# New priority offsets for a planned attention and expert kernel, with the products of batch 2 moved to VectorE

## The chip, the cores and the metric

The kernel runs on one core of a Trainium2 chip. A time is the device time of one execution in microseconds (us). Before the change it is 289.33 us, the median of three runs (289.2, 289.33 and 290.66).

The core has five instruction streams that run side by side and each in their own order: TensorE (PE, with its weight loads shown as PEld), VectorE (DVE), ScalarE (ACT), GpSimd (POOL) and SyncE (SP). SP and POOL also issue transfers between memory and the core; the transfers themselves run on 16 DMA engines.

## What is computed

A gated linear attention feeds a small mixture of four experts. In the reference's words, cut:

```python
# attention: B, H, S, D = 4, 8, 768, 48
f = 1.0 / (1.0 + np.exp(-f_logit))
for t in range(S):
    state = f[:, :, t, :, None] * state + np.einsum('bhd,bhe->bhde', k[:, :, t], v[:, :, t])
    y[:, :, t] = np.einsum('bhd,bhde->bhe', q[:, :, t], state)
# experts: x is y as (B*S, H*D) = (3072, 384); w1 is (4, 384, 1024), w2 is (4, 1024, 384)
p = domain_probs / (domain_probs.sum(-1, keepdims=True) + 1e-09)
for e in range(E):
    h = np.maximum(x @ w1[e], 0.0)
    out += p[:, e:e + 1] * (h @ w2[e])
```

## The kernel before the change

The 768 time steps are cut into six chunks of 128. A chunk holds four batches, each a tile of 128 steps by 8 heads of 48. Inside a chunk the recurrence is written as products of matrices: the gates' logarithms are summed along time on PE, ACT takes exponentials of the sums, q and k are multiplied by these, transposed, and multiplied with each other; the state is carried from chunk to chunk. The result of a chunk (512 rows of x) goes through the four experts. From the second half of chunk 1 on, two experts are handled together in a form with seven products in place of eight. Matrix work is in bf16.

**The plan.** The kernel does not write its order by hand. It declares some 1,470 steps with a priority, a cost for each engine that may run it, its dependencies and the buffers that it takes and frees. `Plan.run` walks through time and gives each engine that is free the ready step of the lowest priority. The list it returns is emitted in that order, and this fixes two things: which engine runs a step that two could run, and the order of the steps on each engine. On the chip an engine executes its steps in that order and waits at the first one that is not ready. `MOVES` is a string of corrections: `q 0.2=3.2` adds 3.2 to the priority of the step named `q 0.2`, and `@DVE` behind a number also binds the step to that engine.

**Names of steps.** The first two numbers are chunk and batch.

- `ld f0.2`, `ld k0.2`, `ld q0.2`: loads of inputs, issued by SP (L282). The loads `v issue 0` to `v issue 3` of chunk 0 and the weight pieces `w issue 0` to `w issue 10` are issued by POOL (L278, L291) and convert to bf16 on the way. `w 0` is one half of expert 0's first matrix (384 KB as bf16), `w 1` the other half, `w 2` and `w 3` those of expert 1, `w 4` and `w 5` the halves of expert 0's second matrix; `w 6` to `w 10` are whole matrices of 768 KB.
- `gate1`, `gate2`, `cs`, `exps`: the gates on ACT, their running sums on PE (L319) and the exponentials `e` on ACT (L339).
- `q 0.2`, `k 0.2`: the products of q and k with the exponentials (L347), on DVE or POOL.
- `tpq`, `tpk`, `ev_tp`: transposes on PE (L356) and their copy out. From batch 2 of chunk 1 on, `tp` is a transposing transfer on SP's queue (L360).
- `at`, `ev_at0`, `ev_at1`, `y`: scores on PE (L383), masked on DVE (L387), and the chunk's result on PE (L394, L398).
- `ev_y`, `xt`, `ev_xt`: in chunk 0 and the first half of chunk 1, the copy of `y`, its transpose on PE and the copy out. Later `ev_ys` scales `y` by the experts' shares (L370 on ACT, L372 on DVE) and `xs` is a transposing transfer on SP's queue (L375).
- `kv`, `ev_kv`, `sf`: the update of the state (PE, DVE, POOL).
- `h 0.1.3.0`: chunk 0, expert 1, hidden block 3: x times w1 on PE (L432); `relu` its eviction (L441, L443). `o 0.1.2.0`: the result of expert 1 for batch 2 from the first half of the hidden blocks (`.1`: from the second half), L447; `ev_o` its eviction, and `store` the transfer to memory (L513).
- `hs`, `relu_s`, `s1` to `s4`, `p`, `ev_p`: the same for pairs of experts (L464, L472, L482, L501, L509 and L271).

**The beginning.** Until chunk 0's attention has made its first x, PE has little to do, and the kernel pads it with matrix products on a constant (L867). `first` is the first `h` step; the number of padding products ahead of each PE step is worked out from the plan's times:

```python
if o.engine == "PE" and o.start <= first:
    o.pad, t = int((o.start - t) / (0.42 if t < 7.0 else 0.25)), o.end
```

**POOL's order in the beginning** is `k 0.0`, `v issue 0`, `q 0.1`, `v issue 1`, `v issue 2`, `q 0.2`, `w issue 0`, `v issue 3`, `w issue 1` and so on to `w issue 9`. `v issue 0` waits for the landing of k of batch 1, `v issue 1` for that of batch 2 (`v_gate`). `w issue 10` waits for the landing of k of chunk 1.

Of the kernel before, what the change touches and what calls it, by code (L numbers as in the profile page):

```python
# [12 lines left out]


MOVES = (
    "q 0.2=3.2;k 0.3=-8.9;ev_y 0.3=-23.3@ACT;cs 1.0=0.8;k 1.0=-0.2;cs 1.1=-4.4;v 1.2=8@ACT;tp 1.2=-43.6;tp 1.3=-25;ev_xt 1.1=24.3;"
    "xs 1.3.1=7.9;ld v2.2=7.4;h 0.0.0.0=-7.3;relu 0.0.0.0=3.1@DVE;relu 0.0.2.0=10.6;relu 0.0.3.0=29@ACT;h 0.0.5.0=6.8;h 0.1.1.0=-16.7;"
    "h 0.1.2.0=-22.6;h 0.1.3.0=-119.1;o 0.1.1.1=4.2;o 0.1.3.0=11.3;h 0.3.2.0=-3.7;relu 0.3.3.0=-13.8@DVE;h 0.3.4.0=-12.9;o 0.2.2.0=28.6;"
    "o 0.2.3.0=-1.9;h 0.3.7.0=39.5;cs 2.1=31.3;tp 2.2=9.1;ev_at1 2.0=17;ev_ys 2.0.0.1=-0@ACT;ev_ys 2.1.1.0=-35.5@ACT;xs 2.1.1=12.6;"
    "ev_ys 2.2.0.1=-0.6@ACT;kv 2.2=48.1;ld k3.0=-2.9;o 0.3.2.1=2.1;store 0.3.0=22.7;h 1.0.0.0=-9.5;relu 1.0.4.0=-0.8@DVE;"  # L20
    "h 1.0.5.0=-42.9;h 1.1.0.0=-50.1;h 1.1.1.0=-41.2;h 1.1.2.0=-4;relu 1.1.2.0=-12.9@DVE;h 1.1.3.0=-41;h 1.1.4.0=-2.3;"
    "relu 1.1.6.0=-44.9@DVE;h 1.2.0.0=-1.9;h 1.2.1.0=-7.4;h 1.2.3.0=-7.1;relu 1.2.4.0=1.6@DVE;h 1.2.5.0=8.6;h 1.3.2.0=8;o 1.2.1.0=10.2;"
    "h 1.3.4.0=-11.3;h 1.3.5.0=-23.7;h 1.3.6.0=-11.9;hs 1.1.0.1.4=-1.2;relu_s 1.1.0.1.4=-9@ACT;hs 1.1.0.1.6=-6.4;hs 1.1.1.1.4=4.8;"
    "exps 3.0=7.9;k 3.1=-3.6;k 3.2=56.5;ev_ys 3.0.0.0=-1.5@DVE;ev_ys 3.0.0.1=0@ACT;ev_ys 3.0.1.0=44.9;ev_ys 3.1.0.0=50.8@DVE;"
    "ev_ys 3.1.0.1=0@ACT;ev_at1 3.2=7.6;ev_ys 3.3.1.0=0.1@DVE;ev_ys 3.3.1.1=6.1@DVE;ev_kv 3.0=23;kv 3.3=9.3;ev_kv 3.3=13.2;"
    "ld q4.0=-11.2;ld k4.2=26.7;ld q4.2=26.5;ev_p 1.1.1.1=6.4;hs 2.0.0.0.2=4.5;p 1.1.1.3=8.6;store 1.2.0=34.8;hs 2.0.0.0.6=-14.7;"
    "hs 2.0.0.1.6=2.4;s3 2.0.0=-32.1;hs 2.0.1.1.0=6.1;hs 2.0.1.0.4=-4.2;hs 2.0.1.1.4=2.8;relu_s 2.0.1.1.4=51.5;p 2.0.1.7=2.6;"
    "p 2.0.1.3=33.7;ev_p 2.0.1.4=-10.5;p 2.1.0.1=1.3;p 2.1.0.2=1.7;hs 2.1.1.0.2=-1.4;hs 2.1.1.1.2=-3.1;p 2.1.0.5=-17.1;"
    "hs 2.1.1.0.6=27.4;hs 2.1.1.1.6=-5.3;s2 2.1.1=-16.6;gate2 4.0=33.9;cs 4.0=-2.3;v 4.1=-8;ev_ys 4.0.0.0=5.6@DVE;ev_ys 4.0.0.1=44@DVE;"
    "xs 4.0.0=-37.1;ev_ys 4.0.1.0=-0@ACT;ev_at1 4.1=1.9;y 4.1=-4.7;ev_ys 4.1.0.1=3.8@DVE;ev_at0 4.3=-29.9;ev_ys 4.3.1.0=-16.5;"  # L30
    "ev_kv 4.1=-1.3;kv 4.2=15.9;ld q5.0=-19.7;ld v5.0=8.7;ld k5.2=25;relu_s 3.0.0.1.0=0.4@DVE;p 2.1.1.6=11.2;ev_p 2.1.1.5=-1.2;"
    "hs 3.0.0.0.4=3.6;relu_s 3.0.0.0.4=8.9@ACT;hs 3.0.0.1.6=-4.9;p 3.0.0.2=3.2;hs 3.0.1.0.2=-1.1;relu_s 3.0.1.0.2=42.4;p 3.0.0.5=-25.6;"
    "p 3.0.0.7=2.1;s3 3.0.1=27.4;hs 3.1.0.1.0=11.9;ev_p 3.0.1.2=13.5;relu_s 3.1.0.1.6=-19.4@ACT;hs 3.1.1.1.0=-27.5;ev_p 3.1.0.2=-4;"
    "hs 3.1.1.1.2=7.5;hs 3.1.1.1.4=-1.8;hs 3.1.1.0.6=-24.3;cs 5.2=-7;cs 5.3=13.5;ev_ys 5.1.0.0=-15;hs 4.0.0.0.0=2.9;"
    "relu_s 4.0.0.0.0=-27.5@DVE;ev_p 3.1.1.1=-15.6;hs 4.0.0.0.2=20.6;p 3.1.1.5=-4.7;hs 4.0.0.1.4=-17.4;hs 4.0.0.1.6=-20.2;"
    "ev_p 4.0.0.3=25.5;s3 4.0.1=-0.4;hs 4.1.1.1.4=16.2;hs 5.0.0.1.2=-13.7;s4 5.0.0=-8.4;hs 5.1.0.1.6=1.5;hs 5.1.1.0.2=-4.8;"
    "hs 5.1.1.1.2=-1.9;relu_s 5.1.1.1.4=-21.2@DVE;s2 5.1.1=14.5"
)


# [98 lines left out]
def kernel(  # L139
# [105 lines left out]
    def tl(kind, *key):  # L245

        if (kind, key) not in tiles:
            room = alias.get(kind, kind if kind in rooms else "ps_m" if kind in inbank else "ps_m")
            slot = P.slot[(room,) + key if kind == room else (room, kind) + key]
            if room in ("gp", "qk", "e"):  # L250
                tiles[kind, key] = pads[room, slot]
            else:
                shape, dt = shapes[kind]
                pool = ps if room.startswith("ps_") else wk
                tiles[kind, key] = pool.tile(shape, dt, name=f"{room}{slot}")
        return tiles[kind, key]

    def after(later, earlier):
        tc.add_manual_dep(later.ins, earlier.ins.name,
                          mybir.DependencyInfo(mybir.DependencyClass.Sync, mybir.DependencyReason.DATA),  # L260
                          reason="order of transfers")
# [4 lines left out]
    def hh(b, n=1):  # L266
        return slice((b % 2) * H, (b % 2 + n) * H)
# [8 lines left out]
    def load(c, nm, b, n):  # L276
        if (c, nm) == (0, "v"):
            ins[c, nm, b] = nc.gpsimd.dma_start(out=tl("vb", c, b), in_=srcs[nm][c, :, b * H:(b + n) * H, :])  # L278
            if b < 2:
                after(ins[c, nm, b], ins[v_gate[b]])  # L280
            return
        ins[c, nm, b] = nc.sync.dma_start(out=tl(nm, c, b // 2)[:, hh(b, n), :],  # L282
                                          in_=srcs[nm][c, :, b * H:(b + n) * H, :])
        if (c, nm, b) == (1, "f", 0):
            after(ins[c, nm, b], ins["w", 6])
        if (c, nm, b) == (1, "f", 1):
            after(ins[c, nm, b], ins["w", w_gate])
# [228 lines left out]
    ld = {}  # L516
    def add_load(c, nm, b, n, prio, deps=(), cost=None):
        op = P.add(f"ld {nm}{c}.{b}", {"DMA": cost or (1.05 if c else 1.1) * n}, lambda e: load(c, nm, b, n), prio,
                   deps=deps, takes=[(nm, c, b // 2)], lag=2.0)
        for i in range(n):  # L520
            ld[c, nm, b + i] = op
        return op


    v_gate, issued = [(0, "k", 1), (0, "k", 2)], []

    def add_v(b, prio):
        issued.append(P.add(f"v issue {b}", {"POOL": 0.8}, lambda _: load(0, "v", b, 1), -600 + b,
                            deps=issued[-1:] + ([ld[v_gate[b]]] if b < 2 else []), takes=[("vb", 0, b)], lag=1.2))
        ld[0, "v", b] = P.add(f"ld v0.{b}", {"DMA": 1.1}, lambda _: None, prio, deps=issued[-1:], lag=2.0)  # L530

    for i, x in enumerate("f0 k0 q0 f1 k1 q1 f2 f3 k2 q2 v0 k3 q3 v1 v2".split()):
        nm, b = x[0], int(x[1])
        if nm == "v":
            add_v(b, -1000 + i)
        else:
            add_load(0, nm, b, 1, -1000 + i)
# [148 lines left out]
    def add_o(c, e, nt, half):  # L686
        p = unit[0] + 0.5
        by_cols = (c, e, nt) == (C - 1, E - 1, B - 1)
        part = half if by_cols else 0
        cols = slice(half * Din // 2, (half + 1) * Din // 2) if by_cols else slice(0, Din)  # L690
        fcs = range(KF) if by_cols else range(half * 4, half * 4 + 4)
        key = ("ps_m", "op", c, e, nt, part)
        d = [hdone[k] for k in hdone if k[:2] == (c, e) and k[2] in fcs and k[3] <= nt * T]
        m = omm[c, e, nt] = P.add(f"o {c}.{e}.{nt}.{half}", {"PE": 0.645}, lambda _: mm_o(c, e, nt, fcs, part, cols), p,
                                  deps=d + (wd[e, 2] if by_cols or len(wd[e, 2]) == 1 else [wd[e, 2][half]]) + [omm.get((c, e, nt))], takes=[key], lag=0.2, frees=[("h", c, e, half_of(c, nt * T))])
        if half == 1 or by_cols:
            w = 0.36 if by_cols else 0.62
            ev = oev[c, e, nt] = P.add(f"ev_o {c}.{e}.{nt}.{part}", {"ACT": 0.58, "DVE": 0.56} if e == 0 else {"DVE": w},
                                       lambda g: ev_o(c, e, nt, part, cols, g), p - 1,
                                       deps=[m, oev.get((c, e - 1, nt)), pdone], takes=[("o", c, nt // 2)], frees=[key])  # L700
            if e == E - 1:
                P.add(f"store {c}.{nt}.{part}", {"DMA": 0.6}, lambda _: store(c, nt, cols), p - 25, deps=[ev], frees=[("o", c, nt // 2)], lag=2.0)
# [32 lines left out]
    def zip_groups(hg, pg, os=()):  # L735
# [73 lines left out]
        for i in range(8):  # L809
            h_unit(i)  # L810
            if i < len(os):
                add_o(*os[i])
            if i == LAG and pg is not None:
                todo.extend((pg, i) for i in range(7))
# [57 lines left out]
YP, RP = 17, 50  # L872
B1, S1, B2, S2 = -10, 4, -2, 6
LAG = 0


# [28 lines left out]
```

## Time and profile before

| what | value |
|---|---|
| runs | 289.2, 289.33, 290.66 us; median 289.33 |
| the profiled execution | 289.56 us, of which the trace's span is 287.8 us |
| granted TensorE clock | 1.000 |
| PE: busy matmul time | 279.7 us, 2982 instructions |
| PEld: weight loads | 234.3 us |
| DVE, ACT, POOL | 193.4, 182.7 and 114.6 us |
| moved by the DMA engines | 41.85 MB, mean 145 GB/s |

The span runs from the first to the last instruction; the time of the execution holds 1.76 us more. A matmul's busy time overlaps that of the next, so the share of 97% does not say that PE streams all the time; the starts of the matmuls in the timeline tell this. Times of events below are counted from the start of the span. A wait in the view of waits is put down to what ended last.

### The profile page before, as it was taken

What the parts mean: (1) busy time and instruction counts of PE and PEld (TensorE: products, weight loads), DVE (VectorE), ACT (ScalarE), POOL (GpSimd) and SP (SyncE); (2) the same over time, 40 slices, a digit from 0 to 9 for tenths busy, and PEclk for the clock granted to TensorE, in tenths of its full rate; (3) what the DMA queues carried; (4) which work ended last, traced back from release to release, by engine and by line L of the source; (5) the groups of instructions that cost most, each with busy time, mean ns of one, the idle gap of its engine ahead of it and who ended that gap; (6) DMA issues with size and microseconds to landing.
All of it is one profiled execution on the core that took longest, in us unless ns stands there. A gap on an engine that the chain in (4) does not pass through costs nothing.

```text
span 287.8 us, 7401 instructions
## 1 busy us (share of the span) xinstructions
PE 279.7 (97%) x2982; PEld 234.3 (81%) x2982; DVE 193.4 (67%) x383; ACT 182.7 (63%) x348; POOL 114.6 (40%) x182
## 2 busy tenths in 40 slices
PE   7989999999999999999999999999999999999994
PEld 2566555567776999999999999999989999999994
DVE  4665232798799758875888879787758830885283
ACT  5857656757766867866676757757657258643630
POOL 5694800429392841678267247306630002000000
PEclk9999999999999999999999999999999999999999
DMA  8999999998979999998999999999374212071101
GB/s 161 199 140 202 208 199 201 185 217 196 176 141 158 188 186 191 169 202 187 184 161 168 175 198 187 197 193 170 63 128 70 44 55 39 6 107 57 56 2 55
DMA packets 157782, 41.85 MB, mean 145 GB/s; under 512 B 148124, under 2 KB 156956, under 8 KB 157748
## 3 DMA queue, kind: packets, MB, share of 16 engines
q1 hardware_dynamic: 146500, 34.66, 65.2%
q0 software_dynamic: 11248, 6.72, 16.8%
q8 instruction: 23, 0.38, 0.5%
q14 instruction: 11, 0.09, 0.1%
HBM read 31.51 MB, written 4.72 MB: 126 GB/s over the span
## 4 chain that ended last, share of the span: by engine, by line
PE 87%; DMA 5%; POOL 2%; SPq 2%; DVE 1%; issue 1%; ACT 0%; DVEq 0%
PE ps_m L464 33%; PE ps_m L501 29%; PE ps_m L432 10%; PE ps_m L447 8%; SPq L282 2%; DMA w_sb<-in_moe_w_dram 2%; PE ps_m L383 2%; DMA x<-yb 1%; DMA k<-in_k_dram 1%; PE ps_m L398 1%; POOL qk L347 1%; PE ps_m L394 1%; PE ps_m L404 1%; PE ps_m L319 1%; POOL vb L278 1%
## 5 line engine op out<-in xcount | busy, mean ns | idle before, releaser
L464 PE MATMUL ps_m<-x,w_sb 128*128 128x256 bf16 x864 | 106.8, 273 | 0.5 <-DMA x<-yb 0.5
L472 ACT ACTIVATE h<-ps_m 128x512 bf16<-128x512 f32 x116 | 69.0, 597 | 45.3 <-PE ps_m L464 41.6
L464 PEld LDWEIGHTS <-w_sb 128*128 128x128 bf16 x864 | 82.6, 98 | 9.5 <-PE ps_m L383 0.6
L509 DVE TENSOR_TENSOR o<-ps_m,o 128x192 f32<-128x192 f32 x91 | 31.5, 354 | 29.5 <-PE ps_m L501 28.1
L501 PEld LDWEIGHTS <-S 128*128 128x128 bf16 x576 | 48.7, 98 | 0.9
L347 POOL TENSOR_TENSOR qk<-q,e 128x384 bf16<-128x384 f32 x20 | 24.4, 1225 | 35.6 <-ACT e L339 34.3
L432 PE MATMUL ps_m<-x,w_sb 128*128 128x256 bf16 (+3 forms) x228 | 36.0, 301 | 1.6 <-DMA w_sb<-in_moe_w_dram 1.3
L501 PEld LDWEIGHTS <-h 128*128 128x128 bf16 x432 | 36.1, 98 | 1.0
L447 PE MATMUL ps_m<-w_sb,h 128*128 128x384 bf16 x192 | 36.3, 326 | 0.0
L482 DVE TENSOR_TENSOR S<-h 128x1024 bf16<-128x1024 bf16 x36 | 25.5, 733 | 13.3 <-ACT h L472 13.3
L419 POOL TENSOR_TENSOR Sf<-Sf,egs 48x192 f32<-48x192 f32 x40 | 20.4, 511 | 31.8 <-DVE Sf L411 25.0
L387 DVE TENSOR_TENSOR AT<-ps_m,mask 128x512 bf16<-128x512 f32 x48 | 30.3, 682 | 3.4 <-PE ps_m L383 3.4
L443 ACT ACTIVATE h<-ps_m 128x512 bf16<-128x512 f32 (+2 forms) x43 | 21.7, 514 | 14.5 <-PE ps_m L432 12.9
L339 ACT ACTIVATE e<-ps_m 128x384 f32<-128x384 f32 x48 | 26.7, 671 | 6.0 <-PE ps_m L319 4.0
L432 PEld LDWEIGHTS <-w_sb 128*128 128x128 bf16 x228 | 20.3, 98 | 11.3 <-DMA w_sb<-in_moe_w_dram 1.8
L501 PE MATMUL ps_m<-ts_sb,S 128*128 128x192 bf16 x288 | 28.8, 246 | 0.0
L501 PE MATMUL ps_m<-w_sb,S 128*128 128x192 bf16 x288 | 28.7, 246 | 0.0
L447 PEld LDWEIGHTS <-h 128*128 128x128 bf16 x192 | 18.4, 98 | 12.2
L501 PE MATMUL ps_m<-w_sb,h 128*128 128x192 bf16 x288 | 27.9, 246 | 0.0
L370 ACT ACTIVATE yb<-ps_m,pn 128x384 bf16<-128x384 f32 x49 | 25.7, 586 | 0.6 <-DVE yb L372 0.4
L271 ACT COPY o<-ps_m 128x192 f32<-128x192 f32 x35 | 11.2, 319 | 21.5 <-PE ps_m L501 21.0
L347 POOL TENSOR_TENSOR qk<-k,e 128x384 bf16<-128x384 f32 x19 | 19.9, 1046 | 11.9 <-ACT e L339 6.3
(74 smaller groups left out, 322.2 us busy)
## 6 DMA issues: line engine op xcount, KB each, us to landing
out_dram<-o SPq DMA_DIRECT2D x23, 192.0 KB, 2.2
w_sb<-in_moe_w_dram POOLq DMA_DIRECT2D x5, 768.0 KB, 17.8
k<-in_k_dram SPq DMA_DIRECT2D x10, 384.0 KB, 6.0
q<-in_q_dram SPq DMA_DIRECT2D x10, 384.0 KB, 5.9
v<-in_v_dram SPq DMA_DIRECT2D x10, 384.0 KB, 5.5
f<-in_f_logit_dram SPq DMA_DIRECT2D x9, 384.0 KB, 4.3
w_sb<-in_moe_w_dram POOLq DMA_DIRECT2D x6, 384.0 KB, 8.2
f<-in_f_logit_dram SPq DMA_DIRECT2D x6, 192.0 KB, 4.0
```

The costliest lines, as they stand in the source:

```text
L339: nc.scalar.activation(out=o, in_=i, func=AF.Exp, scale=1.0 if j else -1.0)
L347: engines[eng].tensor_tensor(out=tl("qk", c, b)[:, j, :, 0:D].rearrange("t (i r) d -> t i r d", r=2), in0=tl("qk"[j], c, b // 2)[:, hh(b), ...
L370: nc.scalar.activation(out=ys, in_=y, func=AF.Copy, scale=pe)
L387: nc.vector.tensor_tensor(out=tl("AT", c, b)[:, r].rearrange("s i t -> s (i t)"), in0=tl("A", c, b, r).rearrange("s i t -> s (i t)"), in1= ...
L432: nc.tensor.matmul(out=hp(c, e, fc, n0, n1, nf)[:, f], lhsT=w1_sb[:, e, kk, (fc + f) * 128:(fc + f + 1) * 128], rhs=tl("xT", c)[:, kk, n0: ...
L443: nc.scalar.activation(out=dst, in_=src, func=AF.Relu)
L447: nc.tensor.matmul(out=tl("op", c, e, nt, part)[:, cols], lhsT=tl("h", c, e, half_of(c, nt * T))[:, fc, nt * T:(nt + 1) * T], rhs=w2_sb[:, ...
L464: nc.tensor.matmul(out=out_[:, f], lhsT=w1_sb[:, e, kk, (fc + f) * 128:(fc + f + 1) * 128], rhs=tl("xs", c, hf, p)[:, el, kk, :], start=(k ...
L472: nc.scalar.activation(out=dst, in_=tl("hp", c, hf, p, el, fc), func=AF.Relu)
L482: nc.vector.tensor_tensor(out=s(j), in0=in0, in1=in1, op=op)
L501: nc.tensor.matmul(out=out_, lhsT=lhs[:, fc, :], rhs=rhs[:, fc, :], start=(first and fc == 0), stop=(fc == KF - 1), skip_group_check=True)
L509: nc.vector.tensor_tensor(out=o, in0=src, in1=o, op=ALU.add)
```

## The change

It replaces the string `MOVES` by another one of the same kind and takes two constants out of the code, whose values stay what they were. No cost, dependency or buffer is touched. The diff, cut; of `MOVES` the first line of the old string stands here, and the first two and the last two of the new one:

```diff
 MOVES = (
-    "q 0.2=3.2;k 0.3=-8.9;ev_y 0.3=-23.3@ACT;cs 1.0=0.8;k 1.0=-0.2;cs 1.1=-4.4;v 1.2=8@ACT;tp 1.2=-43.6;tp 1.3=-25;ev_xt 1.1=24.3;"
...
+    "k 0.1=-21.4;ev_tp 0.1=-1.8@DVE;q 0.2=13.4@DVE;k 0.2=3@DVE;ev_y 0.0=-3.1@DVE;v 1.0=-24.4@POOL;q 1.2=1.3;k 1.3=-11.5;tp 1.3=2.9;"
+    "ev_xt 1.0=1.5@DVE;y 1.1=21.6;ev_ys 1.2.0.0=-7.4@DVE;ev_ys 1.3.1.0=-25.6@ACT;xs 1.3.1=-17.8;ev_kv 1.1=25.3;h 0.0.1.0=-58.2;"
...
+    "hs 5.0.1.1.0=31.4;p 5.0.0.6=3.7;hs 5.0.1.0.4=5.2;relu_s 5.0.1.0.6=-27.8@DVE;p 5.0.1.1=19.1;p 5.0.1.2=46.3;hs 5.1.1.1.6=0.6;"
+    "s2 5.1.1=45.9;p 5.1.1.1=2.2;ev_p 5.1.1.4=-7.5"
 )
...
-            if b < 2:
+            if b < len(v_gate):
...
-    v_gate, issued = [(0, "k", 1), (0, "k", 2)], []
+    v_gate, issued = VG, []
...
-    for i, x in enumerate("f0 k0 q0 f1 k1 q1 f2 f3 k2 q2 v0 k3 q3 v1 v2".split()):
+    for i, x in enumerate(ORDER.split()):
...
 LAG = 0
+ORDER = "f0 k0 q0 f1 k1 q1 f2 f3 k2 q2 v0 k3 q3 v1 v2"
+VG = [(0, "k", 1), (0, "k", 2)]
```

In the program that the new string makes, the steps are the same ones, in another order and partly on another engine:

- DVE has 365 steps in place of 350, ACT 305 in place of 319, POOL 166 in place of 167; PE has the same 489 steps, and 34 padding products in place of 36.
- POOL's beginning is `k 0.0`, `v issue 0`, `k 0.1`, `v issue 1`, `v issue 2`, `w issue 0`, `v issue 3`, `w issue 1` and so on.
- DVE's beginning is `q 0.0`, `ev_tp 0.0`, `q 0.1`, `ev_at0 0.0`, `ev_at1 0.0`, `ev_tp 0.1`, `k 0.2`, `q 0.2`, `ev_at0 0.1`, `ev_y 0.0`, `ev_at1 0.1`, `q 0.3`, `k 0.3`, `ev_at0 0.2`, `ev_at1 0.2`, `ev_y 0.2`, `ev_at0 0.3`, `ev_at1 0.3`, `ev_xt 0.2`. Before, it ran `k 0.1` in place of `q 0.1`, had neither `q 0.2` nor `ev_tp 0.1` nor these `ev_y`, and had `ev_xt 0.0`, which is on ACT now.
- PE runs `y 0.2` ahead of the first `h` step, and that step is `h 0.0.1.0`.
- `o 0.3.0.0` and `o 0.3.0.1` stand behind the other `o` steps of expert 3 and behind `y 1.1`. On SP's queue `store 0.0.0` stands behind `ld f2.0`, and `ld k2.0` behind `store 0.0.0`, `store 0.2.0`, `tp 1.2` and `tp 1.3`; it stood ahead of both `tp`.
- Between chunks 1 and 2, SP's queue has `tp 2.1`, `xs 1.2.0`, `xs 1.2.1`, `tp 2.0`, `xs 1.3.1`, `xs 1.3.0`, `ld k2.2`; it had `tp 2.0`, `xs 1.2.0`, `xs 1.2.1`, `tp 2.1`, `xs 1.3.0`, `ld k2.2`, `ld q2.2`, `store 0.3.0`, `xs 1.3.1`. The first paired step is `hs 1.1.1.0.0` (it reads `xs 1.3.1`) and was `hs 1.1.0.0.0` (it read `xs 1.3.0`).
- At the end PE runs `p 5.0.1.7`, `p 5.1.1.7`, `p 5.0.1.4`; it ended with `p 5.1.1.4`, `p 5.1.1.3`, `p 5.1.1.7`. `p 5.1.1.7` has two evictions, `p 5.0.1.4` one, each followed by a store of 192 KB.

## The prediction

> **What bounds the kernel now.** I read the shares and the chain of waits first, then the waits of PE, then the stretches in which PE does wait.
>
> ```profile
> PE 279.7 (97%) x2982; PEld 234.3 (81%) x2982; DVE 193.4 (67%) x383; ACT 182.7 (63%) x348; POOL 114.6 (40%) x182
> PE 87%; DMA 5%; POOL 2%; SPq 2%; DVE 1%; issue 1%; ACT 0%; DVEq 0%
> ...
> PE ps_m L432 <- DMA w_sb<-in_moe_w_dram: 1.3, 1, 1.3
> PE ps_m L464 <- DMA x<-yb: 0.5, 1, 0.5
> ```
>
> The chain that ended last is PE for 87%. From the first `h` step (19.85) to the last product, the starts of PE's steps in the timeline follow each other at the pace of the products: 0.65 to 0.66 us for each `o`, `hs` and `p`. I found three exceptions: 0.41 us before 22.15 (`ev_xt 0.2` on DVE), 0.07 at 24.5 (weights), and about 0.6 after 91.2, where PE waits for a transposing transfer. Between 92 and 283 no step waits beyond a 0.1 us that each change to the 48-row products of `at` costs. The work of PE is the same after the change, so time can be won or lost in three places only: the beginning, the passage at 91, the tail; and new waits can appear.
>
> The chain in the beginning:
>
> ```profile
> 7.22 4.08 DMA k<-in_k_dram
> ...
> 11.60 1.44 POOL vb L278 x2
> 13.04 0.39 issue
> 13.43 0.95 POOL qk L347
> 14.38 5.42 DMA w_sb<-in_moe_w_dram
> 19.80 0.05 issue
> 19.85 0.50 PE ps_m L432 x3
> ```
>
> Read from below: the first `h` waits for `w 0`, landed at 19.80; that transfer was issued at 14.38, because POOL ran the product `q 0.2` from 13.43. The DMA engines around it, with the columns busy time of PE, PEld, DVE, ACT, POOL, then clock, DMA share and GB/s:
>
> ```profile
> 12.00:13.00 1.00, 1.00 (x6) 0.36 (x4) 0.56 (x1) 1.00 (x3) 1.00 (x2) 1.00 1.27 253
> 14.00:15.00 1.00, 1.00 (x10) 0.70 (x8) 1.00 (x3) 0.44 (x2) 1.00 (x2) 1.00 1.92 100
> 16.00:17.00 1.00, 1.00 (x19) 0.62 (x18) 0.31 (x1) 1.00 (x3) 1.00 (x3) 1.00 0.80 57
> 17.00:18.00 1.00, 1.00 (x14) 0.64 (x10) 0.90 (x2) 0.82 (x3) 1.00 (x2) 1.00 1.27 190
> ```
>
> From 13.6 to 15.7 the engines work through the many 96-byte packets of `v issue 1` and `2` (100 GB/s); then, to about 16.6, hardly a packet starts, and `w 0` flows from 16.6 on. Afterwards the weight pieces keep the engines at some 200 GB/s until 47.6.
>
> **The change, part by part.** ORDER and VG hold the values that stood in the code: nothing.
>
> *POOL's beginning.* `q 0.2` leaves POOL, so `w issue 0` starts at the end of `v issue 2`, 13.43 in place of 14.38, and every later issue with it: 0.95 us. That transfer started to flow 2.2 us after its issue (14.38 to 16.6); from 13.43 this gives 15.65, just as the v packets end. The gap of 0.9 us closes, and all weight pieces land 0.95 earlier. Bounds: 0.95 if the stream moves as a whole; 0 if the engines had no room after all. I take 0.95, for the row of 57 GB/s is nearest to an idle engine.
>
> *Is PE ready for it?* `w 0` would land at 18.85. Batch 1's x must be there. On DVE, `ev_tp 0.1` (0.69 in the row of its kind; ACT took 1.02) ends at about 12.4 in place of 13.17, so `at 0.1` starts at about 13.0, held by five padding products, against 13.22. DVE then needs `k 0.2`, `q 0.2` (0.56 each), `ev_at0 0.1` 0.68, `ev_y 0.0` 0.5, `ev_at1 0.1` 0.68, `q 0.3` and `k 0.3` 1.16, both `ev_at` of batch 2 1.29: 12.4 + 6.0 = 18.4 at most, 17.9 by my closer walk, against 18.39 before. On PE, `y 0.1` waits for `q 0.3`'s transpose ahead of it (about 16.3), `ev_y 0.1` on ACT ends at 17.5, four pads and `xt 0.1` at 18.0, `ev_xt 0.1` (0.48) at 18.75. The first `h` starts at about 18.9, held by `w 0` with 0.1 to spare: a gain of 0.95. Batch 3 comes 0.4 later on DVE (`ev_at1 0.3` at 20.3, 19.86 before).
>
> *Does that last?* The next weight that binds is `w 5`: issued at 19.16, landed 11.6 later, 30.78; the first product that reads it, `o 0.0.0.1`, starts at 30.92 (third in the row at 29.62, two times 0.65). From the first `h` to it PE took 11.07, of which 0.48 waits; now `y 0.2` (0.21) stands ahead, so 10.38 of work remains: 18.9 + 10.38 = 29.28. `w 5` lands at 29.83. So 0.55 us of waits for batches 2 and 3 are covered, and PE goes on at 29.88, 1.04 earlier (0.95, and 0.09 of the slack of 0.14). This is the cover: were the weights 0.55 faster, the later batch 3 would cost what it is late. The same walk with `w 6` to `w 9` leaves 0.7 us or more each. `w 10` is issued at 50.60 after k of chunk 1 and lands 9.0 later, 59.6; `o 0.3.1.0` now comes one `at` (0.43) earlier in the order than the first of its kind did: 60.25 - 0.43 - 1.04 = 58.78, against 59.6 - 0.95 = 58.65. It fits by 0.1; should this piece move by 0.5 only, 0.4 is lost.
>
> [...] While POOL issues `v issue 1` and `2`, DVE now runs two products. In before, `k 0.3` ran beside the issue of `w 0`:
>
> ```profile
> 14.27 0.61 DVE L347 TENSOR_TENSOR qk<-k,e 128x384 bf16<-128x384 f32 x1
> 14.38 0.80 POOL L291 DMA_DIRECT2D w_sb<-in_moe_w_dram  x1
> ```
>
> 0.80 is no more than the other issues take (0.74 to 0.94), so I add nothing. [...]
>
> *Between chunks 1 and 2.* The wait at 91:
>
> ```profile
> 87.33 4.30 DMA x<-yb
> 91.63 0.14 issue
> 91.77 2.78 PE ps_m L464 x24
> ```
>
> `xs 1.3.0` was issued 3.84 ahead of PE's arrival (91.17) and took 4.30 and 0.14 more: 0.60 of wait. After the change the first `hs` needs `xs 1.3.1`. Its chain starts with `y 1.3`, which PE reaches 7.7 us ahead of `at 2.1` (7.2 before), but it needs all four `ev_ys` of that batch, of which the third waits on ACT behind `gate1 2.2` (0.84). Laid out with the rows' durations the issue comes 3.58 ahead of PE: 0.86 of wait, 0.26 more. `tp 2.0` ahead of it has 4.55 to land; the rows of `tp` are 3.1 to 4.8. Bounds: with a landing in 3.1 to 3.4 (the other rows here) there is no wait, 0.60 won; the loss is bounded by the slower rival below. I take 0.26 lost, by the nearest row.
>
> *Engine choices and order from 92 to 283.* Fifteen more evictions on DVE at 0.62 to 0.69: 10 us on an engine that is idle for 94. In each later chunk PE comes to the first use of a transposing transfer 3.4 us or more behind the end of its issue, as before, where this gave no wait. I take 0; bounds 0 and 0.3 lost, half a product.
>
> *Tail.* The last product is followed by one eviction in place of two:
>
> ```profile
> 284.21 0.62 DVE L509 TENSOR_TENSOR o<-ps_m,o 128x192 f32<-128x192 f32 x2 [0.30 <-PE ps_m L501]
> ```
>
> 0.62 - 0.36 = 0.26 won. But `p 5.0.1.7`, `p 5.1.1.7` and `p 5.0.1.4` each wait for the eviction of the step two back: 0.86 from a product's start to its eviction (283.35 to 284.21), 0.36 for that, about 0.1 until PE knows, against 1.32 of PE's own work, and one other eviction queues between: about 0.15 lost. And two stores of 192 KB end together. Net 0.10 won; bounds 0.26 won, 0.2 lost.
>
> *Sum:* -1.04 + 0.26 + 0 - 0.10 = -0.88. On the profiled execution, 289.56, that is 288.68; the median of the runs shown is 0.23 below that execution, so 288.45, said as 288.4.
>
> **The rivals.** *B: the passage at 91 closes.* For it: `tp 2.0` and `xs 1.2.0` landed in 3.1 and 3.4 where fewer transfers stood together, and the loads q, v and f of chunk 2 are issued 2 us earlier. Against it: four transposing transfers follow closely in both orders. -1.04 - 0.60 - 0.26 = -1.9: 287.4.
>
> *C: the change does not do what it says.* The engines show a busy share of 0.80 even at 57 GB/s; if the v packets set the pace, `w 0` stays at 19.80, and 0.26 - 0.10 remain: 289.5.
>
> *D, slower: k of chunk 2.* `ld k2.0` was issued at 66.38, landed in 5.2 us and waited 4.9 for POOL's product at 76.50.
>
> ```profile
> 66.38 1.29 SPq L282 DMA_DIRECT2D k<-in_k_dram  x1
> 69.68 3.34 SPq L360 DMA_TRANSPOSE QK<-qk  x2
> ```
>
> Now it stands behind `store 0.0.0`, which waits for `o 0.3.0.1`: PE reaches its end 7.4 us after 58.8, at 66.2; with the eviction the store goes at 67 to 68, a second one and both `tp` add 3.3: 71. POOL wants `k 2.0` at about 77. Landing in 5.2 gives 76.2, no wait; in the 6.8 of `ld f2.2`, 0.8 late. If the four loads behind each other (1.57 MB) share the 170 GB/s of the stretch 60 to 92, k lands at 80.3, 3.3 late, and behind it on POOL stand `k 2.1`, `q 2.1`, the state and `q 2.0`, for which `tp 2.0` and PE's `at 2.1` wait: 289.33 - 0.88 + 3.3 = 291.7. It decides for slower from a landing at 79.3 on. Against it: q, v and f in that place took 5.6 to 6.8.
>
> **How the numbers follow.** Chances: the forecast 0.43 (its own range 287.9 to 289.3), B 0.30, C 0.09, D 0.18. The range 287.3 to 291.2 leaves out the lower edge of B and the upper half of D. What a measurement of this kernel can tell from no change is about 0.5%, 1.45 us: below 287.88 is faster, above 290.78 slower. Faster: B and 0.04 of the forecast's lower edge, 0.34. Slower: D and 0.04 for a late `w 10` or transfers that add to the loss at 91, 0.22. The rest, 0.44, is no change.
>
> **What would show it.** Right: `w 0` issued at about 13.4 and landed near 18.9, first `h` at 18.9, PE's wait for `w 5` before `o 0.0.0.1` near 29.9, a wait of 0.5 to 1 for x at about 90, one eviction at the end. Wrong: `w 0` still near 19.8; issues on POOL above 1 us; no wait at 90, or one of 2 us or more led by the load of k on POOL; new waits of PE between 92 and 283.

## The result, and where the time went

The changed kernel took 293.65 us (median of 292.25, 293.19, 294.12, 294.19), the kernel before 289.66 beside it on the same chip: ratio 1.0121, 95% interval 1.0095 to 1.0147. By the ratio it is slower by 3.5 us, by the medians by 4.0; the forecast was 288.4, with a range up to 291.2. (Ratios here leave out executions over 1.5% above the fastest of the same kernel.) The profiled execution took 294.19, its span 292.4; it is the slowest of the four, so the profile shows more loss than the median. The page of the changed kernel, with the shares of the engines, the granted clock in 40 slices of 7.3 us, the chain of waits and, of the DMA queues, the one that fetches instructions (packets, MB, share):

```profile
PE 281.7 (96%) x2980; PEld 235.0 (80%) x2980; DVE 203.9 (70%) x398; ACT 175.9 (60%) x334; POOL 116.1 (40%) x181
PEclk9999999999998899999999999999999999999999
q8 instruction: 23, 0.38, 0.5%
PE 83%; DMA 7%; POOL 2%; SPq 2%; DVE 2%; issue 2%; ACT 1%; POOLq 0%; DVEq 0%
```

PE's share of the chain fell from 87 to 83%, and the clock, which was whole before, falls near 93 us. PE's busy time grew by 2.0 us with two padding products fewer; most of that is the half clock, by an estimate from the 3.41 us at 0.50 that are shown below. The waits of PE in the changed kernel, but for one at the very start and the least (total, times, longest):

```profile
PE ps_m L503 <- DVE S L484: 1.3, 1, 1.3
PE ps_m L385 <- DMA QK<-qk: 1.2, 1, 1.2
PE ps_m L434 <- DMA w_sb<-in_moe_w_dram: 1.0, 1, 1.0
PE ps_m L321 <- ACT gp L317: 0.9, 2, 0.6
PE ps_m L466 <- DMA x<-yb: 0.5, 1, 0.5
```

Lines are 2 higher than before. The third and the last answer to the 1.3 and 0.5 shown of before. The first two and the longer part of the fourth are new: for a sum on DVE (at 127), for `tp 2.0` (at 90) and for the gate of chunk 5 (at 176).

Four stretches, cut at the starts of PE's matmuls in the two traces, hold the whole difference of the spans (us). The first matmul starts at 1.52 in both:

| | start to last `o` | last `o` to first `hs` | first `hs` to last `p` | last `p` to the end | span |
|---|---|---|---|---|---|
| name below | head | passage | body | tail | |
| before | 90.36 | 1.40 | 192.16 | 3.90 | 287.82 |
| changed | 89.92 | 2.71 | 196.05 | 3.77 | 292.44 |
| difference | -0.44 | +1.31 | +3.89 | -0.13 | +4.62 |

**Head.** The chain of the changed kernel:

```profile
11.50 1.80 POOL vb L280 x2
13.30 6.43 DMA w_sb<-in_moe_w_dram
19.74 0.05 issue
19.78 0.28 PE ps_m L434
```

`w 0` is issued 1.08 earlier, right behind the two v issues, and lands 0.06 earlier: the transfer takes 6.43 in place of 5.42. It did begin to flow earlier: the 20th packet of weights starts at 15.60 in place of 16.67. But the trace holds 16 landings for this transfer, and PE's first `h` started 0.04 to 0.05 behind the last of them in both kernels (at 19.78 and 19.85): 15 had come by 18.80 (19.64 before) and the last at 19.74 (19.80 before). From `w 5` on the pieces are 0.4 to 0.5 earlier (30.29 against 30.78).

**Passage.** Windows of the changed kernel, columns as in the prediction (busy time of PE, PEld, DVE, ACT, POOL, then clock, DMA share, GB/s):

```profile
89.00:90.00 1.00, 1.00 (x8) 0.53 (x6) 0.37 (x1) 1.00 (x4) 0.58 (x1) 1.00 2.52 89
90.00:91.00 1.00, 0.24 (x2) 0.00 (x0) 0.87 (x2) 0.49 (x2) 0.54 (x1) 1.00 0.05 6
91.00:92.00 1.00, 0.52 (x16) 0.45 (x16) 0.09 (x1) 0.00 (x0) 0.00 (x0) 1.00 0.78 144
93.00:94.00 1.00, 1.00 (x9) 0.75 (x7) 1.00 (x3) 0.45 (x1) 0.00 (x0) 0.62 0.80 149
94.00:95.00 1.00, 1.00 (x6) 0.71 (x5) 0.40 (x1) 0.32 (x2) 0.00 (x0) 0.50 1.24 253
```

Two things are to be seen. From 90 to 91 the transfers move 6 GB/s, while `tp 2.0` and `xs 1.3.1` are in flight: `tp 2.0` lands 5.25 after its issue, `xs 1.3.1` 4.96. The packet records show a fetch of 16,384 bytes of instructions from 88.72 to 90.41, and 18 packets of 256 bytes, begun at 89.26 to 89.58, that all end near 91.3, up to 2.03 us each where one takes 0.02 otherwise. A stretch like this, in which the transfers hardly move, is called a standstill below. And from 93.24 to 96.65, 3.41 us, the clock is 0.50: PE does 6 products from 94 to 95, where it did 12 from 92 to 93 before.

**Body.** Of its 3.89, the half clock is about 1.6, the wait for `s1 2.0.0` 1.51, the gate of chunk 5 0.51, a second sum at 195 0.26. (In the experiments the waits for the sum and the gate are given from one product's start to the next, which makes them 1.62 and 0.62 here.) The sum in the chain, and the load behind the gate:

```profile
126.54 2.56 DVE S L484
...
169.97 5.15 DMA f<-in_f_logit_dram
```

On DVE `s1 2.0.0` ran from 125.43 to 129.09, 3.66 us where its kind takes 0.69, while POOL ran five instructions without a gap. In the timeline it is the second of these two; the others are the first and the last of POOL's five:

```profile
124.51 4.59 DVE L484 TENSOR_TENSOR S<-h 128x1024 bf16<-128x1024 bf16 x2
125.48 0.52 POOL L275 CAST vb<-v 128x384 bf16<-128x384 f32 x1
...
128.49 0.58 POOL L346 DMA_DIRECT2D egs<-e  x1
```

**Tail.** One eviction follows the last product, as forecast (the third of the row; it starts at 288.96):

```profile
288.10 0.82 PE L503 MATMUL ps_m<-ts_sb,h 128*128 128x192 bf16 x8
288.30 1.02 DVE L511 TENSOR_TENSOR o<-ps_m,o 128x192 f32<-128x192 f32 x3 [0.30 <-PE ps_m L503]
```

The theory to be tested: the loss starts with the standstill behind an instruction fetch, which in the changed order holds the transfers that PE needs at once; the wait can bring the half clock, and later waits stand on DVE's sums and on a late load. Its rivals: the four transposing transfers delay each other; the sum is slow by itself; the half clock has another cause; the head is worth what the prediction said. The kernel before was run again beside each group of kernels, on the same chip; every ratio below is to it. Times inside an execution are of its trace, one execution of each kernel.

### The profile page after: what moved, and what is told of

Its sections match the earlier page's. It is cut to its first block, busy times and chain, and to the rows that moved or that the text cites. A ratio compares the mean times of both kernels' runs of the same rounds, so it can differ in the third digit from the quotient of the medians.

```text
span 292.4 us, 7388 instructions
## 1 busy us (share of the span) xinstructions
PE 281.7 (96%) x2980; PEld 235.0 (80%) x2980; DVE 203.9 (70%) x398; ACT 175.9 (60%) x334; POOL 116.1 (40%) x181
## 3 DMA queue, kind: packets, MB, share of 16 engines
q0 software_dynamic: 11248, 6.72, 16.6%
## 4 chain that ended last, share of the span: by engine, by line
PE 83%; DMA 7%; POOL 2%; SPq 2%; DVE 2%; issue 2%; ACT 1%; POOLq 0%; DVEq 0%
PE ps_m L466 30%; PE ps_m L503 26%; PE ps_m L434 11%; PE ps_m L449 10%; DMA w_sb<-in_moe_w_dram 2%; SPq L284 2%; DMA f<-in_f_logit_dram 2%; DMA x<-yb 2%; DVE S L484 2%; PE ps_m L385 2%; PE ps_m L400 1%; DMA k<-in_k_dram 1%; PE ps_m L396 1%; PE ps_m L406 1%; PE ps_m L321 1%
## 5 line engine op out<-in xcount | busy, mean ns | idle before, releaser
L474 ACT ACTIVATE h<-ps_m 128x512 bf16<-128x512 f32 x114 | 67.1, 598 | 46.1 <-PE ps_m L466 34.2
L511 DVE TENSOR_TENSOR o<-ps_m,o 128x192 f32<-128x192 f32 x91 | 30.7, 354 | 25.0 <-PE ps_m L503 21.7
L421 POOL TENSOR_TENSOR Sf<-Sf,egs 48x192 f32<-48x192 f32 x40 | 22.5, 563 | 44.0 <-DVE Sf L413 42.5
L484 DVE TENSOR_TENSOR S<-h 128x1024 bf16<-128x1024 bf16 x36 | 31.2, 891 | 7.3 <-ACT h L474 7.2
L449 PE MATMUL ps_m<-w_sb,h 128*128 128x384 bf16 x192 | 35.3, 326 | 0.0
L349 POOL TENSOR_TENSOR qk<-q,e 128x384 bf16<-128x384 f32 x18 | 23.1, 1287 | 26.9 <-ACT e L341 14.3
L445 ACT ACTIVATE h<-ps_m 128x512 bf16<-128x512 f32 (+2 forms) x48 | 23.4, 497 | 16.5 <-PE ps_m L434 15.5
L349 POOL TENSOR_TENSOR qk<-k,e 128x384 bf16<-128x384 f32 x20 | 22.1, 1107 | 15.6 <-ACT h L474 5.5
L472 DVE TENSOR_SCALAR h<-ps_m 128x512 bf16<-128x512 f32 x30 | 20.3, 690 | 9.4 <-PE ps_m L466 7.2
L372 ACT ACTIVATE yb<-ps_m,pn 128x384 bf16<-128x384 f32 x44 | 23.7, 587 | 4.3 <-PE ps_m L400 2.3
```

The lines of the kernel that those rows point to most:

```text
L349: engines[eng].tensor_tensor(out=tl("qk", c, b)[:, j, :, 0:D].rearrange("t (i r) d -> t i r d", r=2), in0=tl("qk"[j], c, b // 2)[:, hh(b), ...
L372: nc.scalar.activation(out=ys, in_=y, func=AF.Copy, scale=pe)
L445: nc.scalar.activation(out=dst, in_=src, func=AF.Relu)
L449: nc.tensor.matmul(out=tl("op", c, e, nt, part)[:, cols], lhsT=tl("h", c, e, half_of(c, nt * T))[:, fc, nt * T:(nt + 1) * T], rhs=w2_sb[:, ...
L474: nc.scalar.activation(out=dst, in_=tl("hp", c, hf, p, el, fc), func=AF.Relu)
L484: nc.vector.tensor_tensor(out=s(j), in0=in0, in1=in1, op=op)
```

## The experiments

**The fetch.** In all traces the 16 KB fetches stand on average 126 of PE's products apart, each product being two PE instructions, counted from the start, paddings included; they are taken here for the fetches of PE's own instructions. By that count, more and smaller padding products ahead of the first `h` should move a fetch against PE's work and leave the steps' order as it is. The first of these kernels (e1):

```diff
+    split = 25
     for o in done:
         for _ in range(o.pad):
-            nc.tensor.matmul(out=spare, lhsT=busy[:, 0:128], rhs=busy, start=True, stop=True)
+            if o.name == "cs 0.0" or not split:
+                nc.tensor.matmul(out=spare, lhsT=busy[:, 0:128], rhs=busy, start=True, stop=True)
+                continue
+            split -= 1
+            for _ in range(4):
+                nc.tensor.matmul(out=spare[:, 0:112], lhsT=busy[:, 0:128], rhs=busy[:, 0:112], start=True, stop=True)
```

> The changed kernel with 25 of the padding products ahead of the first h split into four of 112 columns each: 75 more products, 150 more PE instructions, before the first h, all else as it was. Theory (a 16 KB fetch of instructions, one for some 255 PE instructions in the traces, is followed by a standstill of all transfers): the fetch of 88.7 comes 150 instructions earlier, at about 80.5, and the next one at about 94.5; transfers flow between 89.3 and 91.2; tp 2.0 lands 3.1 to 4.2 after its issue in place of 5.25; the wait before at 2.1 is under 0.3 in place of 1.30, the granted clock stays 1.00 behind it; time about 290.5. Rival (four transposing transfers close behind each other delay each other): 5.25 and the wait of 1.30 stay, time within 0.7 of 293.65.

Ratio 0.9995 (0.9961 to 1.0029), median 290.23. The fetches stood at 82.16 and 95.10. Windows:

```profile
89.00:90.00 1.00, 1.00 (x8) 0.59 (x6) 0.43 (x1) 1.00 (x3) 0.03 (x1) 1.00 0.97 190
90.00:91.00 1.00, 1.00 (x15) 0.54 (x14) 0.75 (x2) 1.00 (x2) 0.54 (x1) 1.00 0.64 125
```

The transfers go on, PE doesn't wait; passage 0.81, body 192.16: the same as the kernel before. The four transposing transfers are as close to each other as in the changed kernel, so that rival falls. That the time fell by all of the loss, not only by the passage and the half clock, was not expected; the sums below tell why.

The control with the unaltered changed kernel, and the first attempt at a placebo (e5: six products of 72 columns for each of the 25 paddings):

> The changed kernel once more, unaltered, beside the others on the same chip. Both theories: ratio to the kernel before within 1.0095 to 1.0147; in the profile a 16 KB fetch at 88 to 91, a standstill of the transfers behind it, body (first hs to last p) 193 to 196 against 192.16 in the kernel before.

> The changed kernel with the same 25 padding products split into six of 72 columns each: 125 more products, 250 more PE instructions, nearly one whole fetch period (some 255), so that the fetches come back to where they were. Theory (the place of the fetch decides): a fetch at 87.5 to 91, a standstill behind it, tp 2.0 or xs 1.3.1 landing 4.8 or more after the issue, passage (last o to first hs) 2.2 to 3.2 as in the changed kernel (2.71), body over 193, ratio to before about 1.010. Rival (the finer padding itself, by another head, made the earlier run faster): no wait, passage 0.8, body 192.2, ratio about 1.000.

The control: ratio 1.0151 (1.0095 to 1.0207); fetch at 93.53, standstill 93.86 to 95.29, passage 2.41, body 194.89. Both lie outside what was expected, the ratio by 0.0004 and the fetch by 2.5 us. The fetch stands at PE's product 721, as it did (720), but all of it comes later: this execution waited 1.97 for `w 10` at 61.5, and its half clock followed there (62.78 to 66.20), not behind the passage. The placebo missed: ratio 0.998 (0.9941 to 1.0019), passage 0.81. Its fetch came at 91.63, behind the first `hs` (90.82), so its trace agrees with both theories and it decides nothing: the seventh fetch had stood at product 872, not at 720 + 125. A second one was laid out by that count:

```diff
+            for _ in range(7):
+                nc.tensor.matmul(out=spare[0:64, 0:64], lhsT=busy[:, 0:64], rhs=busy[:, 0:64], start=True, stop=True)
```

> The changed kernel with the 25 padding products split into seven of 64 columns each: 150 more products. In ten traces the sixth fetch inside the span stood at PE's product 710 to 731, paddings counted, and the seventh, with paddings split, at 869 to 873; so the seventh now falls on the kernel's own product 721, where the sixth of the changed kernel falls (720). Theory (place of the fetch): fetch at 88 to 91, a standstill behind it, passage 2.2 to 3.2, body over 193.5, ratio to before 1.009 to 1.015 although the padding is the finest of all. Rival (fine padding itself helps): passage 0.81 and ratio about 0.999 as in the two runs with split padding.

Fetch at 86.44 (2 us earlier than laid out), standstill 87.05 to 88.71, passage 2.81, body 194.16, with the waits for the sum (1.62) and the gate (0.62) back: in the trace the loss returns with the finest padding of all, and the rival that fine padding itself helps falls there. The ratio, 1.0022 (0.9992 to 1.0051), missed what was expected: the executions lie between 289.7 and 294.2 with one at 296.55, median 292.11, which is 1.0059 of the median before. The fetch's place differs by some 30 products between traces, and this kernel sits where it hits in a part of them; that reading of the spread is argued, not shown.

All 17 traces together say the same. Between the issue of the first of the transposing transfers ahead of the passage and the first `hs`, 12 traces hold 14 or more small packets of over 0.9 us, and their passage is 1.25 to 3.15 (1.37 to 3.15 with the changed order, 1.25 to 1.66 with the one before). Five hold three at most, and their passage is 0.81 or 0.82 in either order.

**The half clock.** Six products ahead of `at 2.1` and two ahead of `hs 1.1.1.0.0`, into banks that are written anew (e2):

```diff
+        for _ in range({"at 2.1": 6, "hs 1.1.1.0.0": 2}.get(o.name, 0)):
+            bank = tl("A", 2, 0, 0).rearrange("s i t -> s (i t)") if o.name == "at 2.1" else tl("hp", 1, 1, 1, 0, 0)
+            nc.tensor.matmul(out=bank, lhsT=w1_sb[:, 0, 0, 0:128], rhs=w1_sb[:, 0, 1, 0:512], start=True, stop=True)
         o.emit(o.engine)
```

> The changed kernel with six products of 512 columns ahead of at 2.1 and two ahead of hs 1.1.1.0.0, which fill PE's two waits and write banks that the next products write anew. Theory (the clock falls to 0.5 because PE stood still for some 2 us): granted clock 1.00 from 92 to 97, hs steps 0.655 in place of 1.28, time about 1.5 less than the changed kernel's 293.65, so 292.1. Rival (the fall comes from something else that happens at 93): clock 0.5 for about 3.4 us as before, time 293.65 or up to 0.3 more.

The clock stayed at 1.000 in all 7 executions (the changed kernel: 0.992 to 0.998 in its first four), and the windows behind the passage show it:

```profile
93.00:94.00 1.00, 1.00 (x19) 0.64 (x14) 0.84 (x2) 0.00 (x0) 0.00 (x0) 1.00 1.27 194
94.00:95.00 1.00, 1.00 (x11) 0.90 (x10) 1.00 (x3) 0.42 (x1) 0.00 (x0) 1.00 1.24 217
```

This agrees with idle time as the cause of the half clock; the windows in the last section say it better, for executions with a clock of 0.995 or less are only two of four in each of the changed kernel's runs, and some kernels whose trace shows little or no wait there have them too (e1 3 of 10, e13 3 of 12). The ratio was 1.0109 (1.0072 to 1.0145), hardly under the control's: body 194.81, with 1.61 for the sum, and 1.28 at the gate where it had been 0.6. The control, whose body had the full clock too, has nearly the same (194.89, with 1.61 and 1.36). So the half clock is a part of the loss in some executions, and filling the waits won nothing clear of noise.

**The sums.** `s1` and `s2` of 2.0.0 ahead of `s3` (e3), in the list of steps behind `P.run()`; the load of the next experiment is moved in the same way:

```diff
     done = P.run()
+    at_ = {o.name: o for o in done}
+    for name, ahead in [('s1 2.0.0', 's3 2.0.0'), ('s2 2.0.0', 's3 2.0.0')]:
+        done.remove(at_[name])
+        done.insert(done.index(at_[ahead]), at_[name])
```

> The changed kernel with s1 2.0.0 and s2 2.0.0 issued on DVE ahead of s3 2.0.0. Theory (a sum that runs beside POOL's products ends only when POOL's unbroken run ends; the first of the row gets through in 1.0): s1 takes about 1.0 and the next sum some 3.7; p 2.0.0.5 doesn't wait, p 2.0.0.6 waits 0.2 at most for s2; time 1.3 less than 293.65, so 292.35. Rival (s1 itself is slow, by its operands): s1 takes over 3 us in first place too, and no time is won or up to 0.3 lost.

Ratio 1.0088 (1.0055 to 1.0121), median 292.44. DVE in the timeline (start, duration):

```profile
124.88 0.81 DVE L484 TENSOR_TENSOR S<-h 128x1024 bf16<-128x1024 bf16 x1
125.72 3.54 DVE L484 TENSOR_TENSOR S<-S,h 128x1024 bf16<-128x1024 bf16 x1
```

The second sum is now the slow one, whichever it is, and PE has no wait at 127, so the rival falls that `s1` is slow by its operands. POOL tells why e1 lost nothing here without this edit. In e1 POOL waited for its load of v, and `s1` ended in the gap:

```profile
122.00 0.58 POOL L346 DMA_DIRECT2D egs<-e  x1
123.39 0.50 POOL L275 CAST vb<-v 128x384 bf16<-128x384 f32 x1 [0.82 <-DMA v<-in_v_dram]
```

Where PE is 2 us late (the changed kernel, e2, e8, e9, the control), v has landed by then, POOL's eight instructions leave no gap for 6 us (122.80 to 129.07 in the changed kernel), and the sum there ends only at 129.09, 0.56 behind the end of the seventh, a cast begun at 128.04. In e3 the passage cost 3.13 and yet the clock didn't fall, see the last section.

**The late load.** `ld f5.0` ahead of `tp 4.1` on SP (e9):

> The changed kernel with ld f5.0 ahead of tp 4.1 on SP: issued at about 167.7 in place of 169.97. Theory (cs 5.0 waits for f of chunk 5, which is issued behind a transposing transfer that waits for POOL and then stands still behind a fetch): the wait before cs 5.0 (0.5 to 1.36 in four traces) is gone, s1 2.0.0 and the passage stay as they are; time 0.5 to 1.2 less than the changed kernel's, ratio 1.007 to 1.012 where the changed kernel has 1.012 to 1.015. Rival (gate1 5.0 on ACT is late by ACT's own queue): the wait stays.

Ratio 1.0081 (1.0054 to 1.0108). No wait at the gate; passage 2.65 and 1.62 for the sum stay. In the changed kernel the load was issued at 169.97, with a fetch at 170.11 and a standstill from 170.38 to 172.04. The ratio's interval overlaps the changed kernel's: the trace shows that the wait is gone, the time alone would not.

**What each is worth.** Both of these edits without the padding (e12), and with the padding of e1 (e10, again as e13):

> The changed kernel with s1 2.0.0 and s2 2.0.0 ahead of s3 2.0.0 and ld f5.0 ahead of tp 4.1; the padding is left as it is. Theory (three losses that add: passage 1.3 to 2 and sometimes the half clock's 1.5; the sum 1.6; f 0.5 to 1.3): passage 2.4 to 3.1, body 192.2 to 192.6 unless the clock falls, ratio 1.003 to 1.006, halfway between the mended kernel (0.9975) and the changed one (1.012 to 1.015). Rival (the two waits are only the same lateness told again, so that mending them moves it elsewhere): ratio 1.008 or more.

> The changed kernel with the padding split into four (75 more products), s1 2.0.0 and s2 2.0.0 ahead of s3 2.0.0, and ld f5.0 ahead of tp 4.1. Theory: passage 0.81, body 192.2 in the profile, ratio 0.995 to 0.999: the change's own order is worth about 0.3 to 1 us less than the kernel before once its three waits are gone. Rival (new collisions of fetches with other transfers take their place): ratio 1.000 to 1.004.

> The mended kernel (padding split into four, sums moved, ld f5.0 moved) once more. Theory: ratio 0.995 to 0.9995 again, passage 0.81, body 192.1 to 192.5. Rival (the first interval was luck): 1.000 or more.

e12: 1.0066 (1.0034 to 1.0098), passage 3.15, body 192.54. e10: 0.9975 (0.9955 to 0.9996), passage 0.82, body 192.14. e13: 0.9994 (0.9971 to 1.0018), passage 1.37, for its fetch stood at 84.36 with a standstill to 86.86. So, in ratios: from 1.0136 (mean of the changed kernel's two) to 1.0066 for the sum and the load, 2.0 us; from there to 0.9985 (mean of e10 and e13) for the passage, 2.3 us. These are not prices that hold by themselves: e1, with the padding alone and neither edit, was at 0.9995 already, so in these runs the sum and the load cost PE something only when it is late. e12 came out just above what was expected; 4 of its 12 executions have a granted clock of 0.994. With its three waits mended, the change is level with the kernel before; the first run's lead did not hold in the second.

**The head alone.** The kernel before with `q 0.2` on DVE (e4, again as e11), and the kernel before unaltered with its profile (b0):

```diff
+    for name, ahead in [('q 0.2', 'ev_at0 0.1')]:
...
+    for name, engine in [('q 0.2', 'DVE')]:
+        at_[name].engine = engine
```

> The kernel before with q 0.2 on DVE (behind k 0.2) in place of POOL, all else as it was: the head of the change alone. The step of the prediction: w 0 is issued at 13.43 and lands at 18.9, time 0.95 less than the kernel before, 288.7 against 289.66. Rival (what stands in the transfer engines ahead of w 0, not its issue, sets its landing): w 0 lands at 19.6 to 19.8, later pieces 0 to 0.5 earlier, time 0 to 0.45 less, 289.2 to 289.66.

> The kernel before with q 0.2 on DVE once more. Theory of the first run (fewer slow executions, a lower median by 0.8): ratio 0.995 to 0.999 again and no time over 291.5. Rival (the first interval was luck): ratio 0.999 to 1.002, times up to 292.5 as before has them.

> The kernel before, unaltered, with a profile from this chip. All theories: ratio 0.998 to 1.002. For the gain of q 0.2 on DVE: either first h to last o takes longer here than with q 0.2 on DVE (70.4 and 70.9), by 0.3 to 0.8, or the waits of the passage are longer than 1.25 and 1.66.

In e4 k of batch 2 landed late, so all of POOL's beginning was later, but the distances tell:

```profile
12.57 1.80 POOL vb L278 x2
14.38 6.33 DMA w_sb<-in_moe_w_dram
```

6.33 from the issue to the landing, as in the changed kernel. In 17 traces the first `h` comes 5.7 to 6.8 us (median 6.3) behind the end of `v issue 2` where `q 0.2` is on DVE, and 6.2, 6.4 and 7.3 where it stands between on POOL. The issue of `w 0` moves by 0.95. Its first part lands 4.63 behind that point in place of 5.43 (medians of 14 and 3 traces), its 15th 5.82 in place of 6.21, its last 6.11 in place of 6.38. So the earlier issue brings the first parts forward by nearly what it should, and the last, for which PE waits, by some 0.3. What holds the last parts is not shown; the 96-byte packets of v are a candidate, for in the changed kernel those of `v issue 3` run from 17.5 to 19, between those of `w 0`.

Still the time fell: 0.9967 (0.9946 to 0.9988) and 0.9976 (0.9955 to 0.9996), 1.0 and 0.7 us, 0.8 in the mean; it is the one version here whose interval lay below 1 in both of its runs. b0 was 1.000 (0.9978 to 1.0023) and shows a part: behind its wait for `w 0` (1.90 of standing in one window, see the last section) the clock was 0.5 from 20.61 to 24.02. Of 121 executions of the kernel before on the four chips of the experiments 17 have a granted clock of 0.995 or less, with a median of 292.0 against 290.4 for the others; of the 22 of e4 and e11 none has (of the ten of e7 below, one). In the mean that is 0.2 of the 0.8. The rest isn't explained: b0 took 71.9 from the first `h` to the last `o`, e4 and e11 70.4 and 70.9, but its half clock alone costs some 1.7 there (an estimate, half of the 3.41 us), and it ran on another chip than they did; passage (1.65, there 1.25 and 1.66), body and tail are the same.

**Padding on the kernel before** (e6), and both of its gains together (e7):

> The kernel before with 25 padding products split into four of 112 columns: its fetch of 88.65 comes 150 instructions earlier. Theory: passage 0.81 in place of 1.40 (no wait for x), body 192.2, no half-clock stretch in any run; time 0.6 less than before by the passage, up to 1.0 less with the half-clock stretches gone: ratio 0.9965 to 0.998. Rival (the fetches now hit other transfers that bind): body over 192.5, ratio 1.000 or more.

> The kernel before with q 0.2 on DVE and with the padding split into four: both single gains together. Theory (they add): ratio 0.9967 of the first and 0.9965 to 0.998 of the second, so 0.993 to 0.995, 288.5 to 289.0 where before takes 290.5, faster than both kernels. Rival (both gains are the same: fewer runs with a half-clock stretch): 0.996 to 0.997.

e6: 1.0003 (0.9975 to 1.0031); the passage did fall to 0.81, but one execution still had a half clock and the rest was taken up elsewhere (1.18 of wait at 23.8 in its head). e7: 0.9981 (0.9949 to 1.0013), passage 0.81. They don't add; the expectation for both was too good.

## Why the prediction was wrong, by its steps

- **The head, forecast 0.95 to 1.04 won.** Measured 0.06 at the first `h`, 0.45 at `o 0.0.0.1`. "That transfer started to flow 2.2 us after its issue (14.38 to 16.6); from 13.43 this gives 15.65" came about true: the 20th packet of weights starts at 15.60, where it stood at 16.67. The step that failed is the next, "The gap of 0.9 us closes, and all weight pieces land 0.95 earlier": 15 of 16 parts of `w 0` came 0.8 to 1.2 earlier, the last 0.06. A stream that starts earlier was taken for one whose last part lands earlier by as much. The bounds had 0 as one end, and rival C, at 0.09, had the landing right; its reason, the v packets, is a candidate. (The gap itself may have had another cause than the one read: a fetch of instructions ran from 15.68 to 16.62 in before, just there. This was not tested.)
- **DVE beside POOL.** The prediction added nothing for DVE's two products beside the issues of POOL, and rightly: the two v issues took 1.82 with both products beside them (1.83 with one before), `w issue 0` 0.76 (0.80). The cost stood in another place, where DVE adds two tiles: in the 17 traces 98 of these sums took over 1.2 us (0.69 is what the kind takes otherwise), and each ended 0.54 to 0.56 behind the end of an instruction of POOL. For 82 it was the first of POOL's to end in their time, for 16 a later one, among them the eight of 3.5 to 3.7 us (`s1 2.0.0` here), which ended behind the fourth of an unbroken row. Why these ended no sooner is open.
- **The passage, forecast 0.26 lost.** Measured 1.31, and about 1.6 for the half clock. The step that failed is "`tp 2.0` ahead of it has 4.55 to land; the rows of `tp` are 3.1 to 4.8": it had 4.05 and took 5.25. The transfer of 4.30 in before was taken for ordinary; it had stood still for 1.7 us behind a fetch (88.65), and the next order put two needed transfers there. No case held the half clock.
- **The body, forecast 0 with 0.3 as bound.** Measured 3.89, with the half clock's 1.6. The step that failed is "Fifteen more evictions on DVE at 0.62 to 0.69: 10 us on an engine that is idle for 94", with "I take 0": DVE's work was costed by its idle time over the whole stretch. The sums, which the step left out, met POOL's run (1.51 and 0.26), and the load of f a standstill (0.51). The evictions as such cost nothing: e1 has them all, and its body took 192.16 as before.
- **Rival D** had the sign and, at 291.7, the size nearest, but not the cause: `ld k2.0` landed at 76.91, 1.9 us after POOL began to wait for it, but POOL then waited 0.75 more for ACT, and the products behind came some 0.2 later than before.
- **The tail, 0.10 won**, was right in size: 0.13.

That PE would wait near 90 for transfers, and longer than before, was foreseen; what was wrong was to take rows of single transfers as bounds without asking what had made one of them slow.

## What to carry to other kernels

Where one transfer takes 1 to 2 us more than its kind, look in the packet records for a standstill before using its row as a price: the 4.30 in before held one of 1.7 us. It need not stay with that transfer. In the changed order `tp 2.0` (5.25) and `xs 1.3.1` (4.96) were in flight at the standstill, and with 75 more products ahead (e1) the fetch of 88.72 came at 82.16 and the passage fell from 2.71 to 0.81. A transfer that starts to flow earlier need not land earlier by as much: `w 0` flowed 1.07 earlier, and its last part landed 0.06 earlier. A wait of PE that fits in a range can still double: the passage lost 1.31, and the half clock that followed 1.76 us of standing in one window lost about 1.6 more. And a sum on DVE beside an unbroken row of POOL instructions took 3.66 us, where its kind takes 0.69.

## What the runs showed of the hardware

- **Standstills.** In 17 traces there are 398 fetches of 16 KB. Where a transposing transfer had been issued in the 2 us ahead, 95 of 128 were followed within 2 us by a standstill (six or more small packets of over 0.9 us each); issued 2 to 4 us ahead, 23 or 24 of 64, by how the edges are taken; neither, 0 of 206. The other way round, of 124 such groups of packets in these traces 120 begin between 0.5 ahead of a fetch and 2.2 behind it. In one trace the standstill began 0.4 ahead of the fetch, so which holds which is open; fetches without a transposing transfer in the 4 us ahead showed none (the 0 of 206).
- **The clock's windows.** The records of the granted clock, but for the last of each trace, have lengths that are multiples of 3.413 us. By that grid, in all 17 traces: 21 windows in which PE stood still for 1.0 to 1.74 us were followed by the full clock, and the three with 1.75, 1.76 and 1.90 (the control, the changed kernel, b0) by one window of 0.5, as were all windows with 2.25 or more, which lie at the end. The ends of products are modelled, so the edge is known to some 0.1 at best. This fits e3 too, which stood still for longer in sum (1.35 and 0.83 on the two sides of a window's edge) and kept its clock. So in these traces the half clock followed from 1.75 us of standing in a window of 3.41, about half of it. The window ahead of the half clock in the changed kernel (PE was busy for 1.65 of it):

```profile
89.83:93.24 3.41, 1.65 (x25) 1.06 (x24) 2.37 (x5) 0.66 (x2) 0.67 (x2) 1.00 0.49 82
```
